# First batch of a frequency-filter and mixer kernel: filter loads on two other queues, tables issued earlier, second token weights added up on GpSimd

## The chip, the cores and the metric

The kernel runs on one core of a Trainium2 chip. The metric is the device time of one execution in microseconds. The engines are TensorE (PE for its matmuls, PEld for its weight loads), VectorE (DVE), ScalarE (ACT), GpSimd (POOL) and SyncE (SP), which only issues DMAs here. ACT and POOL can issue DMAs too; the issue stands in the engine's own instruction stream. "SPq", "ACTq" and "POOLq" are issues on these engines' queues.

## The reference

Eight batches `x[b]` of 3008 rows by 256 columns. Each is filtered in the frequency domain along the rows, then passes a token mixer and a channel mixer. Inputs are given in double precision words of 64 bits where numpy made them so (the four mixer weights); the kernel turns these into 32 bits itself.

```python
X = np.fft.rfft(x, axis=1)
Y = X * (filt_r + 1j * filt_i)[None]
x = np.fft.irfft(Y, n=3008, axis=1)
xt = x.transpose(0, 2, 1)
h = np.maximum(xt @ w_tok1, 0) @ w_tok2        # 3008 -> 256 -> 3008
u = x + h.transpose(0, 2, 1)
out = u + np.maximum(u @ w_ch1, 0) @ w_ch2     # 256 -> 1536 -> 256
```

## The kernel before

**The stages.** One group is one batch. The transform of length 3008 = 47 x 64 is done in two stages of matmuls. For batch 0, `dft(GROUPS[0])` does the following, all on the chip:

- Twelve `a_unit`s (columns in two halves, rows in six chunks) multiply an x tile with the table `wa0` (L518), and ACT copies the result into `turned` (L521). After each six of them `turn_back` transposes that half of `turned` on DVE.
- Eight steps c0 to c7, one for four of the 32 frequencies of the inner transform. In a step, `b_turned(c)` multiplies with the table tile `wb` into two banks; `products(c)` (L676) multiplies both banks with the filter tile `filt` on DVE; `bi_turned(c)` multiplies back with the same `wb` and with `negs`, a negated piece of the table that `negate(c)` (L238) makes on ACT; and ACT copies the result into `turned` again (L662). L505 is the helper `four` which holds the matmuls of both.

After the steps `turn_back` transposes `turned` once more, and PE forms the first token product (`token_sums`, L765). `token_relu` (L841, ACT) takes it up, `u_unit` (L859) multiplies with the second token weights `w2`, and from there on the loop `mix` runs all eight batches through the mixer, with the transforms of the next batch spread between by a table of due places.

**The weights.** The 64-bit weights come as raw words in tiles `st` and are converted by `halves`: ACT scales the upper words (L258), DVE works on the bits (L260, L261, L264, L266), and the two parts `top` and `rest` are added up. Either PE adds them, as two matmuls with an identity-like table (`on_chip`, L304 and L305), and ACT copies the sum out (L307); or `rounded` adds them on DVE (L293). There are 38 such tiles, in this order:

- 12 tiles of the first token weights `w1` (`w1_tile`), all loaded by SP (`i < EARLY`), two halves each. Added by PE.
- 14 tiles of the second token weights, `w2_load(0)` to `w2_load(13)`, seven for each half of the 256 token channels. Tiles 0 to 5 of each seven have 470 columns, the last 188; the target is written with 128 columns between its elements. Loaded by POOL (L340). `BY_PE = 10`: tiles 0 to 9 are added by PE, tiles 10 to 13 by DVE.
- 12 tiles of the channel weights `wc`, loaded by POOL, added by DVE, two of them before `mix` begins.

Each tile is a generator with stages load, ACT's part, DVE's first part, DVE's second part and addition. Four pointers walk over the list: `begin` (load), `copy` (ACT), `middle`, `end`; `convert()` moves the last three by one and begins loads up to five tiles ahead.

**The order.** Everything is written out by hand (`manual_schedule`): the program order on each engine is the order of the calls. In the steps of batch 0 the generator yields four times a step, and two tiles of `w1` are converted per step; then each `convert()` with `w2` tiles goes along with one of four pieces of `token_sums`.

**Loads of batch 0.** All x tiles are issued at first, half by SP, half by POOL. The filter is loaded by `filt_quad(c)`: for the real part `filt_r` and the imaginary part `filt_i`, two rows groups `odd` = 0 and 1, each with one load of 24 rows by two of 256 (48 KB, L227) and one of 23 rows backwards (46 KB, L230); c0 has the second one in two pieces (L232 and L233). There are three filter tiles `filts` and, for batch 0, two more from the pool `t2`, which are zeroed by POOL. `table_load(c)` loads a table tile of 256 KB (L557) on SP. In before, SP issues in this order: table c0, filter c0 (both parts), the table of c1, then in each step `filt_r` of a step three ahead and the table of a step two ahead, and between them the `w1` tiles. `filt_i` from c1 on is issued by POOL.

Of the kernel before, what the change touches and what calls it, by code (L numbers as in the profile page):

```python
# [14 lines left out]
ALU = mybir.AluOpType  # L15
# [9 lines left out]
K2 = 32  # L25
# [11 lines left out]
KD = 2 * KC  # L37
# [10 lines left out]
MT = 6  # L48
NG = 10
W2G = -(-N2 // NG)  # L50
BY_PE = 10
AP = A // 2
W1S = 7
IN_B = 16
# [74 lines left out]
def kernel(  # L129
# [11 lines left out]
    nc = tc.nc  # L141
# [59 lines left out]
    filts = [glob.tile([P, 2, KC, D], FP32, name="filt%d" % i) for i in range(FB)]  # L201
# [17 lines left out]
    def raw(src, row, ap):  # L219
        return bass.AP(tensor=src.tensor, offset=src.offset + row * D, ap=ap)  # L220

    def filt_quad(c, tiles=filts, queues=(nc.sync, nc.sync)):
        t = tiles[c % len(tiles)]
        for i, (q, src) in enumerate(zip(queues, (filt_r, filt_i))):
            for odd in range(KC):
                k, to = c * KD + odd, odd * HALF
                q.dma_start(t[to:to + A, i], raw(src, k, [[64 * D, A], [KC * D, 2], [1, D]]))  # L227
                down = t[to + 32:to + 32 + A]
                if k:
                    q.dma_start(down[0:A - 1, i], raw(src, 64 - k, [[64 * D, A - 1], [-KC * D, 2], [1, D]]))  # L230
                else:
                    q.dma_start(down[:, i, 0], raw(src, 32, [[64 * D, A], [1, D]]))  # L232
                    q.dma_start(down[0:A - 1, i, 1], raw(src, 64 - KC, [[64 * D, A - 1], [1, D]]))  # L233
# [3 lines left out]
    def negate(c, wb):  # L237
        nc.scalar.activation(out=negs[:, c % 4], in_=wb[:, :, 2], func=AF.Copy, scale=-1.0)  # L238
# [4 lines left out]
    late = [(t2p, "t2"), (t3p, "t3")]  # L243
    stages = [(t4p, "t4")] * (A // 2) + (early * 3)[0:TC * W2G + DH] + late * 5

    def stage(n):
        where, tag = stages.pop(0)
        return where.tile([P, n], I64, tag=tag, name="st")

    def halves(st, n, pair):  # L250

        words = [st.bitcast(t).rearrange("p (n w) -> p n w", w=2)[:, 0:n] for t in (U32, FP32)]
        lo, hi, hi_f = words[0][:, :, 0], words[0][:, :, 1], words[1][:, :, 1]
        top, rest = (v[:, 0:n] for v in pair)
        top_i, rest_i = top.bitcast(U32), rest.bitcast(U32)


        nc.scalar.activation(out=top, in_=hi_f, func=AF.Copy, scale=2.0 ** -112)  # L258
        yield
        nc.vector.tensor_scalar(out=top_i, in0=top_i, scalar1=3, scalar2=None, op0=ALU.logical_shift_left)  # L260
        nc.vector.scalar_tensor_tensor(out=top_i, in0=hi, scalar=0x80000000, in1=top_i,  # L261
                                       op0=ALU.bitwise_and, op1=ALU.bitwise_or)
        yield
        nc.vector.tensor_scalar(out=rest_i, in0=top_i, scalar1=0xFF800000, scalar2=None, op0=ALU.bitwise_and)  # L264

        nc.vector.scalar_tensor_tensor(out=rest, in0=lo, scalar=2.0 ** -52, in1=rest, op0=ALU.mult, op1=ALU.mult)  # L266
        yield top, rest
# [3 lines left out]
    def spare_pair():  # L271
        where, tag = spare[0]
        spare.append(spare.pop(0))
        both = where.tile([P, 2, 512], FP32, tag=tag, name="both")
        return both[:, 0], both[:, 1]
# [3 lines left out]
    def rounded(st, n, parts, late):  # L279
        if late:  # L280

            late_in.reverse()
            where, tag = late_in[0]
            both = where.tile([P, 2, 512], FP32, tag=tag, name="both")
            pair = both[:, 0], both[:, 1]
        else:
            pair = spare_pair()
        h = halves(st, n, pair)
        yield next(h)
        yield next(h)  # L290
        top, rest = next(h)
        for src, dst in parts():
            nc.vector.tensor_tensor(out=dst, in0=src(top), in1=src(rest), op=ALU.add)  # L293


    ended = [0]
# [2 lines left out]
    def on_chip(stat, top, rest, n, parts):  # L299
        banks.append(banks.pop(0))  # L300

        def f(tag=banks[0]):
            ps = bank(tag)
            nc.tensor.matmul(ps[:, 0:n], stat, top, start=True, stop=False)  # L304
            nc.tensor.matmul(ps[:, 0:n], stat, rest, start=False, stop=True)  # L305
            for src, dst in parts:
                nc.scalar.copy(out=dst, in_=src(ps))  # L307

        behind.append(f)

    def w1_tile(i):
        st = stage(512)
        rows = moe_w_tok1.rearrange("(n2 n1) t -> n2 n1 t", n1=N1)
        q = nc.sync if i < EARLY else nc.gpsimd
        last = 2 * i + 2 == A
        if last:
            nc.gpsimd.memset(st.bitcast(U32)[HALF:P, 512:1024], 0)
        for h in range(2):
            n = 1 if last and h else 2
            lo = h * A + 2 * i  # L320
            src = rows[:, lo:lo + n, :]
            if h == 0:
                src = bass.AP(tensor=rows.tensor, offset=rows.offset + (A - 1 - lo) * DT,
                              ap=[[N1 * DT, N2], [-DT, n], [1, DT]])
            q.dma_start(st[h * HALF:(h + 1) * HALF, 0:n * DT].rearrange("p (a t) -> p a t", t=DT), src)
        yield

        h = halves(st, 512, spare_pair())
        yield next(h)
        yield next(h)  # L330
        on_chip(wai_t, *next(h), 512, [(lambda v: v, w1[:, 2 * i:2 * i + 2, :].rearrange("p a t -> p (a t)"))])

    def w2_load(i):

        t, g = divmod(i, W2G)
        nn = min(NG, N2 - g * NG)
        n = nn * N1

        st = stage(512)
        nc.gpsimd.dma_start(st[:, 0:n], moe_w_tok2[ts(t, P), ds(g * NG * N1, n)])  # L340
        yield
        dst = w2[:, t].rearrange("p (a h n2) -> p h n2 a", h=2, n2=HALF)[:, :, ds(g * NG, nn), :]

        def some(h, first, step, w):
            return (lambda v: bass.AP(tensor=v.tensor, offset=v.offset + first, ap=[v.ap[0], [N1, nn], [step, w]]),
                    dst[:, h, :, 0:w])

        parts = [some(0, A - 1, -1, A), some(1, A, 1, A - 1)]
        if i < BY_PE:
            h = halves(st, n, spare_pair())  # L350
            yield next(h)
            yield next(h)
            on_chip(ident, *next(h), n, parts)
        else:
            yield from rounded(st, n, lambda: parts, False)

    def combine(w):
        a11, a12, s4, na22, s3, s2, s1 = (w[:, :, n, :] for n in range(7))
# [22 lines left out]
    def wc2_load(i):  # L381
# [11 lines left out]
        while put_off:  # L393
# [7 lines left out]
    tiles = ([w1_tile(i) for i in range(A // 2)] + [w2_load(i) for i in range(TC * W2G)]  # L401
             + [wc1_load(c * (DC // 512), False) for c in range(DH)] + [f(i) for f, i in LAST])
# [147 lines left out]
    def dft(bs):  # L550
        first = bs[0] == 0
        nb = len(bs)
        tiled = bs not in GROUPS[0:2]
        todo = [(b, c) for b in bs for c in range(NXC // 2 if tiled else NXC)]
        wbs = {}

        def table_load(c):  # L557
            where, tag = (t1p, "t1") if first and c % 5 > 2 else (wbp, "wb")
            wbs[c] = where.tile([P, 2, 4, HALF], FP32, tag=tag, name="wb")
            nc.sync.dma_start(wbs[c], (wbi0_d if first else wbi_d)[:, ts(c, 2)])  # L560
# [4 lines left out]
        def w_load(c):  # L565
            table_load(c)
            filt_quad(c)

        to_load = list(enumerate(todo))

# [40 lines left out]
                    next_sum()  # L611
            yield "w"
        for i, u in enumerate(() if tiled else todo):
            if first and i == 0:
                w_load(0)
            if first and i == 6:
                table_load(1)
            a_unit(*u)
            if bs != GROUPS[1] or i >= XB:
                more(1)  # L620
            yield "a" if i + 1 < len(todo) else "w"
            if first and (i + 1) % (NXC // 2) == 0:

                turn_back(i // (NXC // 2))
# [77 lines left out]
                    w_load(c)  # L702
        yield "w"
        yield "b"
        last = K2 // KD
        if not first:
            for c in range(last):
                pss = b_sets(c)
# [8 lines left out]
                yield "i" if c + 1 == last else "b"  # L717
            bi_sets(last - 1, turn)
            return
        tiles = list(filts)  # L720
        for i in range(2):
            t = t2p.tile([P, 2, KC, D], FP32, tag="t2", name="filt")
            nc.gpsimd.memset(t, 0.0)
            tiles.append(t)

        def filt_next(c):
            if c < last:
                filt_quad(c, tiles, (nc.sync, nc.gpsimd))

        filt_next(1)  # L730
        negate(0, wbs[0])
        filt_next(2)
        pss = b_turned(0)
        for c in range(last):
            products(c, pss, tiles)
            if c + 1 < last:
                pss = b_turned(c + 1)
            bi_turned(c)
            yield
            filt_next(c + 3)  # L740
            yield
            if c + 2 < last:
                table_load(c + 2)
            yield
            if c + 1 < last:
                negate(c + 1, wbs[c + 1])
            yield
# [468 lines left out]
    with tc.manual_schedule():  # L1216
# [29 lines left out]
        parts = [(e, part) for e in range(DH) for part in range(2)]  # L1246
# [33 lines left out]
        n = MT * JP  # L1280
# [58 lines left out]
```

## Time and profile before

| | us |
|---|---|
| median of 3 runs | 2452.27 |
| lowest, highest | 2447.38, 2452.76 |
| profiled execution | 2449.51 |
| its span | 2447.7 |
| PE busy | 2357.9 (96%) |
| DVE busy | 1946.9 (80%) |
| ACT busy | 664.4 (27%) |
| POOL busy | 609.3 (25%) |

The span is the time from the first to the last instruction of the profiled execution; the rest of its time, 1.8 us, lies around it. The granted clock of TensorE in that execution was 0.984 on average. In the windows view each row is one stretch of the span, with the busy time of each engine and the number of its instructions. In the chain and timeline views, the first number is the start in us, the second the length; a bracket tells the idle time before and which engine, line or DMA ended it. In the view of waits, a row tells who waited on what, for how many us in all, in how many places, and the longest one.

The stages of batch 0 in this execution: the last copy of line 521 ends at 21.30; the products of c0 to c7 begin at 28.24, 48.99, 65.69, 76.08, 92.14, 105.16, 116.31 and 122.88; PE works on the token product from 134.8 to 160.9; the relu is at 176.72; and the loop `mix` has begun by 185.

### The profile page before, as it was taken

To read this page: it belongs to the slowest core of one execution; us is meant where nothing else is said; L and a number is where in the kernel's file an instruction comes from. 1 tells how busy PE (TensorE), PEld (TensorE's weight loads), DVE (VectorE), ACT (ScalarE), POOL (GpSimd) and SP (SyncE) were. 2 spreads that over 40 slices of the span, in tenths; PEclk is the share of its full clock that TensorE was granted. 3 is DMA by queue.
4 is the path that set the end of the run, shared out by engine and by line. 5 is a ranking of instruction groups with operands and counts; after the bars stand their busy time and mean duration, and the time that the engine had idled before them with its cause. 6 is when DMAs were issued, how large, how long until landed. Compare 5 with 4: busy or idle time off the path is not lost.

```text
span 2447.7 us, 37536 instructions
## 1 busy us (share of the span) xinstructions
PE 2357.9 (96%) x13436; PEld 1998.9 (82%) x13436; DVE 1946.9 (80%) x3645; ACT 664.4 (27%) x1313; POOL 609.3 (25%) x1047
## 2 busy tenths in 40 slices
PE   3778999999999999999999999999999999999998
PEld 1356788988888888988889888888889888898887
DVE  4579877778887788778887788877887788877786
ACT  2343222232222222132222322222222322212222
POOL 5137535112112311221211121123112212112122
PEclk7899999999999999999999999999999999999999
DMA  7545344633345333533335333443335333431100
GB/s 160 136 127 168 112 132 134 219 122 95 106 127 171 116 92 101 190 112 104 97 116 189 116 90 105 140 160 113 93 103 188 118 97 100 122 128 28 41 14 21
DMA packets 186886, 288.05 MB, mean 118 GB/s; under 512 B 35658, under 2 KB 122612, under 8 KB 186700
## 3 DMA queue, kind: packets, MB, share of 16 engines
q1 hardware_dynamic: 148796, 230.09, 30.0%
q0 software_dynamic: 35008, 52.12, 8.2%
q10 hardware_dynamic: 2896, 3.44, 0.4%
q8 instruction: 106, 1.74, 0.3%
q14 instruction: 80, 0.66, 0.1%
HBM read 205.91 MB, written 79.58 MB: 117 GB/s over the span
## 4 chain that ended last, share of the span: by engine, by line
PE 90%; DVE 4%; issue 1%; ACT 0%; DMA 0%; POOL 0%; DVEq 0%; POOLq 0%; ACTq 0%
PE ps_po L986 35%; PE ps_pg L952 19%; PE ps_pg L968 15%; PE ps_b L505 3%; PE ps_b L816 3%; PE ps_acc L873 3%; PE ps_acc L816 2%; PE ps_b L873 2%; PE ps_pg L505 2%; PE ps_b L851 2%; PE ps_acc L851 2%; PE ps_b L765 1%; DVE t L930 1%; DVE both L261 0%; DVE hh L930 0%
## 5 line engine op out<-in xcount | busy, mean ns | idle before, releaser
L994 POOL DMA_DIRECT2D out_dram<-r x752 | 408.9, 551 | 1450.6 <-issue 817.5
L973 ACT ACTIVATE hh<-hh 128x512 f32<-128x512 f32 (+1 forms) x576 | 347.7, 621 | 1013.8 <-DVE hh L930 1009.9
L930 DVE TENSOR_TENSOR hh<-ps_pg,s 128x512 f32<-128x512 f32 (+3 forms) x864 | 481.9, 585 | 170.8 <-ACT s L955 160.8
L986 PE MATMUL ps_po<-t,wc 128*128 128x256 f32 (+1 forms) x2296 | 558.0, 380 | 0.7 <-DVE t L930 0.7
L986 PEld LDWEIGHTS ps_po<-t,wc 128*128 128x128 f32 x2296 | 427.9, 190 | 95.2 <-issue 38.7
L952 PE MATMUL ps_pg<-v,wc 128*128 128x256 f32 (+1 forms) x1728 | 413.6, 375 | 0.1
L986 PE MATMUL ps_po<-hh,wc 128*128 128x256 f32 (+1 forms) x1722 | 411.5, 375 | 0.6 <-POOL wc L364 0.6
L952 PEld LDWEIGHTS ps_pg<-v,wc 128*128 128x128 f32 x1728 | 328.8, 190 | 38.5 <-POOL wc L363 0.7
L986 PEld LDWEIGHTS ps_po<-hh,wc 128*128 128x128 f32 x1722 | 326.8, 190 | 38.5 <-POOL wc L364 1.4
L968 PE MATMUL ps_pg<-u,wc 128*128 128x256 f32 (+1 forms) x1152 | 292.1, 376 | 5.0 <-DVE hh L930 4.9
L930 DVE TENSOR_TENSOR t<-t,hh 128x256 f32<-128x256 f32 (+1 forms) x576 | 245.9, 427 | 19.8
L968 PEld LDWEIGHTS ps_pg<-u,wc 128*128 128x128 f32 x1152 | 217.2, 190 | 36.3 <-DVE hh L930 10.3
L930 DVE TENSOR_TENSOR s<-ps_pg,hh 128x512 f32<-128x512 f32 (+1 forms) x288 | 196.1, 681 | 30.7 <-DVE hh L930 0.9
L955 ACT COPY s<-ps_pg 128x256 f32<-128x256 f32 (+1 forms) x288 | 106.0, 368 | 332.2 <-PE ps_pg L952 331.0
L930 DVE TENSOR_TENSOR t<-hh 128x512 f32<-128x512 f32 (+1 forms) x288 | 194.1, 674 | 0.6 <-ACT hh L973 0.6
L952 PE MATMUL ps_pg<-u,wc 128*128 128x256 f32 (+1 forms) x576 | 169.9, 377 | 4.2 <-DVE hh L930 4.2
L968 PE MATMUL ps_pg<-v,wc 128*128 128x256 f32 (+1 forms) x576 | 169.2, 375 | 0.0
L952 PEld LDWEIGHTS ps_pg<-u,wc 128*128 128x128 f32 x576 | 108.3, 190 | 19.9 <-DVE hh L930 7.8
L968 PEld LDWEIGHTS ps_pg<-v,wc 128*128 128x128 f32 x576 | 109.2, 190 | 13.0
L676 DVE TENSOR_TENSOR p<-ps_acc,filt 128x1024 f32<-128x1024 f32 x64 | 77.7, 1214 | 33.9 <-PE ps_b L505 21.6
L930 DVE TENSOR_TENSOR u<-ps_acc,u 128x256 f32<-128x256 f32 (+1 forms) x84 | 46.1, 549 | 72.9 <-PE ps_acc L873 50.4
L930 DVE TENSOR_TENSOR u<-ps_b,u 128x512 f32<-128x512 f32 (+2 forms) x126 | 74.5, 591 | 28.9 <-PE ps_b L873 26.7
(153 smaller groups left out, 2640.1 us busy)
## 6 DMA issues: line engine op xcount, KB each, us to landing
w<-w_tmp SPq DMA_DIRECT2D x84, 448.0 KB
w<-w_tmp SPq DMA_DIRECT2D x35, 896.0 KB
out_dram<-r POOLq DMA_DIRECT2D x696, 32.0 KB, 3.5
g_tmp<-t SPq DMA_DIRECT2D x224, 96.0 KB
t<-g_tmp SPq DMA_DIRECT2D x42, 512.0 KB
t<-z_tmp SPq DMA_DIRECT2D x196, 96.0 KB
z_tmp<-t SPq DMA_DIRECT2D x72, 256.0 KB
wb<-wbi_t SPq DMA_DIRECT2D x64, 256.0 KB
```

What stands on the lines that cost most here:

```text
L505: nc.tensor.matmul(outs(i, j), stat(i, j), mov(i, j), start=start, stop=stop)
L676: nc.vector.tensor_tensor(out=prods[c, h], in0=pss[h].unsqueeze(1).to_broadcast([P, 2, 2, D]), in1=tiles[c % len(tiles)], op=ALU.mult)
L816: nc.tensor.matmul(ps[:, at], w[:, n], mov, start=(j == 0 and i in (0, 2)), stop=(j == AP - 1 and i >= 5))
L851: nc.tensor.matmul(ps[:, ds(q * P, n)], t4[b, c][:, r, ts(dh, P)], wai[:, 0:n], start=(first and q == 0), stop=(not first and q == 3))
L873: nc.tensor.matmul(ps[:, ds(j * hw, hw)], h1[:, n, :], w2m[m % 2][:, at, 0:hw], start=(i < 2 and j == 0), stop=(j == len(todo) - 1))
L930: nc.vector.tensor_tensor(out=out, in0=in0, in1=in1, op=op)
L952: nc.tensor.matmul(ps[:, 0:hw], chan[0][:, jp, n, :], mov, start=True, stop=True)
L955: nc.scalar.copy(out=s[:, 0], in_=g[0][:, 0, 0:hw])
L968: nc.tensor.matmul(ps[:, 0:hw], chan[0][:, jp, n, :], mov, start=True, stop=True)
L973: nc.scalar.activation(out=hs, in_=hs, func=AF.Relu)
L986: nc.tensor.matmul(po[i][:, j, 0:hw], chan[1][:, jp, n, :], mov, start=(jp == 0 and first == 1), stop=(jp == JP - 1 and last == 1))
L994: q.dma_start(bass.AP(tensor=ob.tensor, offset=ob.offset + row * D + g * cw, ap=[[N1 * D, 32], [D if h else -D, n], [1, cw]]), blocks[ts(g ...
```

## The change

Three things. First, the constant `BY_PE` goes from 10 to 6, and `rounded` is told by `late=None` to add on GpSimd: so w2 tiles 6 to 13, eight tiles, are added there, and PE adds only tiles 0 to 5. Second, batch 0's filter loads go out with `filt_r` on ScalarE's queue and `filt_i` on GpSimd's, c0's too; and c1's are issued in the middle of the `a_unit`s, no longer after them. Third, the tables of c0 and c1 are issued before the first and the third `a_unit`, c2's before the steps, and then each step issues the table of the step three ahead, on SP, before the filter of the same step.

The lines move a little: in the changed file the products are L684, `table_load`'s DMA L562, the addition of `rounded` L294, the filter loads L227, L230, L232 and L233 as before, and the relu L843.

```diff
-BY_PE = 10
+BY_PE = 6
...
         top, rest = next(h)
+        q = nc.vector if late is not None else nc.gpsimd
         for src, dst in parts():
-            nc.vector.tensor_tensor(out=dst, in0=src(top), in1=src(rest), op=ALU.add)
+            q.tensor_tensor(out=dst, in0=src(top), in1=src(rest), op=ALU.add)
...
-            yield from rounded(st, n, lambda: parts, False)
+            yield from rounded(st, n, lambda: parts, None)
...
+        last = K2 // KD
...
+        tiles = list(filts)
+
+        def filt_next(c):
+            if c < last:
+                filt_quad(c, tiles, (nc.scalar, nc.gpsimd))
...
-            if first and i == 0:
-                w_load(0)
-            if first and i == 6:
-                table_load(1)
+            if first and i in (0, 2):
+                table_load(i // 2)
+            if first and i in (0, 6):
+                filt_next(i // 6)
             a_unit(*u)
...
-        tiles = list(filts)
         for i in range(2):
             t = t2p.tile([P, 2, KC, D], FP32, tag="t2", name="filt")
             nc.gpsimd.memset(t, 0.0)
             tiles.append(t)
 
-        def filt_next(c):
-            if c < last:
-                filt_quad(c, tiles, (nc.sync, nc.gpsimd))
-
-        filt_next(1)
+        table_load(2)
+        filt_next(2)
         negate(0, wbs[0])
-        filt_next(2)
         pss = b_turned(0)
         for c in range(last):
...
             yield
+            if c + 3 < last:
+                table_load(c + 3)
             filt_next(c + 3)
             yield
-            if c + 2 < last:
-                table_load(c + 2)
             yield
```

More of the change, by code (lines that the diff above doesn't have):

```diff
@@ L704, in dft @@
         yield "b"
-        last = K2 // KD
         if not first:
```

## The prediction

> **What bounds the kernel now.** First the windows view, to see where PE is not full (columns: length, busy us of PE, PEld, DVE, ACT, POOL, granted clock, DMA share, GB/s).
>
> ```profile
> 0.00:25.00 25.00, 14.04 (x24) 4.63 (x24) 12.79 (x12) 8.32 (x13) 15.16 (x26) 0.96 0.85 188
> 25.00:125.00 100.00, 55.24 (x404) 28.35 (x404) 50.10 (x73) 25.71 (x62) 25.70 (x34) 0.74 0.59 140
> 125.00:185.00 60.00, 46.11 (x288) 33.30 (x288) 41.27 (x78) 24.92 (x49) 19.88 (x37) 0.91 0.43 121
> 185.00:265.00 80.00, 69.52 (x288) 49.82 (x287) 74.72 (x124) 25.68 (x48) 64.75 (x93) 0.98 0.48 153
> 265.00:2447.00 2182.00, 2172.98 (x12436) 1882.77 (x12436) 1768.05 (x3361) 579.73 (x1141) 483.81 (x859) 1.00 0.37 115
> ```
>
> From 265 us PE is full, so what the prologue saves or loses carries to the end. All edits lie before 185. Between 25 and 125, the eight DFT steps c0 to c7, every engine is half idle. The waits of that stretch, then the start of VectorE's product in some of the steps:
>
> ```profile
> ACT turned L662 <- PE ps_pg L505: 50.2, 6, 21.8
> ...
> PE ps_acc L505 <- DMA wb<-wbi_t: 43.7, 5, 18.4
> ```
> ```profile
> 28.24 1.23 DVE L676 TENSOR_TENSOR p<-ps_acc,filt 128x1024 f32<-128x1024 f32 x1 [2.29 <-PE ps_b L505]
> ...
> 48.99 1.22 DVE L676 TENSOR_TENSOR p<-ps_acc,filt 128x1024 f32<-128x1024 f32 x1 [12.32 <-DMA filt<-in_filt_r_dram]
> ...
> 105.16 1.23 DVE L676 TENSOR_TENSOR p<-ps_acc,filt 128x1024 f32<-128x1024 f32 x1 [2.21 <-PE ps_b L505]
> ...
> 116.31 1.22 DVE L676 TENSOR_TENSOR p<-ps_acc,filt 128x1024 f32<-128x1024 f32 x1
> ...
> 122.88 1.22 DVE L676 TENSOR_TENSOR p<-ps_acc,filt 128x1024 f32<-128x1024 f32 x1
> ```
>
> PE waits for tables, DVE once for a filter. c1 to c5 take (105.16-48.99)/4 = 14.0 us each; c6 to c7, with nothing late, 6.6, which is DVE's own work. So the steps are bound by loads. Now the loads themselves (SyncE's queue, then 5 us of the windows view):
>
> ```profile
> 45.77 2.08 SPq L227 DMA_DIRECT2D filt<-in_filt_r_dram  x1
> 47.89 0.32 SPq L230 DMA_DIRECT2D filt<-in_filt_r_dram  x1
> 48.25 2.21 SPq L227 DMA_DIRECT2D filt<-in_filt_r_dram  x1
> ```
> ```profile
> 45.00:50.00 5.00, 0.32 (x1) 0.00 (x0) 1.00 (x1) 1.34 (x3) 1.97 (x3) 1.00 0.27 69
> ```
>
> A pair of filter loads (94 KB) leaves every 2.4 us, though the DMA engines are 27% busy on average: something narrower than sixteen engines is full. After the steps, the chain of waits:
>
> ```profile
> 160.90 0.79 PE ps_po L304 x2
> ...
> 166.56 1.33 POOL st L372 x3
> ...
> 171.45 4.61 DMA filt<-in_x_dram
> 176.06 0.66 ACT both L258
> 176.72 0.49 ACT h L841
> ```
>
> PE ends the token sums at 160.9, but the relu of line 841 starts at 176.72: it stands on ACT behind the conversion of a channel-weight tile (L258) whose load POOL issued only at 166.56.
>
> **Part 1: the start.** In the changed program ACT issues five filter loads of c0 before its table load (1.28 us), each behind the first x loads (landing 5 to 9 us by the x loads' waits), so the first copy (7.32 now) comes near 10. Then four loads of c1 stand between the sixth and the seventh copy of `turned`; the last needs the semaphore lane of the first half of w1 tile 0. By that landing some 4.3 MB must have moved (x 3.1, c0's filter 0.4, table 0.26, w1 piece 0.26, some of c1); at the 188 GB/s of the first window that is 22 us, where the seventh copy starts at 14.01 now. Six copies at the present 1.1 us follow, so the last ends near 27.5 instead of 21.3: c0 late by 6 us. Nothing covers it (DVE's transposes wait for these copies), unless the loads would have been late anyway.
>
> **Part 2: the loads of the steps.** Removed from SP's queue: 28 loads of filt_r in c1 to c7, and ten of c0. Each cost 0.23 to 0.31 us of issue but up to 3.13 us of blocked queue, with the tables behind them. The tables of c2 and c3 now go out before w1 tile 5. Added to ACT: 33 issues of about 0.33 us (its one DMA issue, wai_t, took 0.34), 1.3 us a step, beside PE's and DVE's work. They wait for landings; behind them on ACT stand two L258 for DVE, the copy L307, `negate` and the next `turned` copies, for which PE and DVE wait. POOL gets five i-loads of c0, 0.6 to 1.1 us each, after its x loads, before the memsets of two tiles; c1's and c2's follow, with 5 us of slack.
>
> If queues were the bound, the floor is DVE: c0 at 34.5, then 7 x 6.9 (products 2.4, two w1 tiles at 2.25 each) puts c7 at 83. [...] The last filter lands near 101, products of c7 at 104: 19 us earlier than 122.88. By the queue reading it is 40 earlier. I take 19, since the even share of c6 and c7 already ran at DVE's pace; the 6 us of part 1 are inside, as the loads go on during it. Ends: 40, and -11 (the rival below).
>
> **Part 3: the w2 tiles.** Tiles 6 to 9 leave PE (four passes of 0.79 us in two rows, 1.6 a tile, 6.3 in all) and ACT (L307, 0.97 a tile); 10 to 13 leave DVE (1.0 a tile). POOL adds eight tiles, six of 240+230 columns and two of 96+92. The nearest row is its own 128x256 add,
>
> ```profile
> L900 POOL TENSOR_TENSOR w<-w 128x256 f32<-128x256 f32 x15 | 12.3, 818 | 18.0 <-DMA w_tmp<-w 14.7 <-PE ps_pg L505 2.5
> ```
>
> 0.82: 6 x 1.64 + 2 x 0.9 = 11.6 us; the write steps over 128 columns, which that row lacks, so up to twice, 23. It spreads over about 20 us in which POOL only issues 0.55 us loads, so it hides; but loads queue behind adds that wait for DVE, the channel tile's above all. What it buys: DVE's conversion of w2 tiles 8 to 13 no longer waits for PE between token sums. From c7's product, DVE is done with transposes at +15.6 and PE puts tile 5 through near +26.5; tiles 8, 9, 10 end at +29, +31, +34, POOL's add at +36, the channel load issues by +38 and lands by +45 (7 to 9 us now), relu at +46 instead of 176.72-122.88 = +53.8. That is 7 us; at most 15 (relu right after the sums at +38), at worst -4 if the strided adds lag.
>
> **Sum.** 19 + 7 = 26 us off the profiled 2449.51: 2423.5. That run lies 2.8 us under the median, so 2426.3.
>
> **Rivals.**
> - Queues, not one engine, were the bound: c7 at 83, 40 + 7 = 47 us, 2405. For: 43.7 us of table waits with tables behind filter loads on SP. Against: the 27% row. 20%.
> - The split does nothing for the steps (same eight semaphore lanes for SP and ACT, nine loads a step): only part 3, 7 us, 2445. 14%.
> - Slower: ACT becomes the bound. All its work stands behind loads for three steps ahead, which wait for w1 loads, which wait for ACT's conversions. It decides where a step from c0 at 34.5 exceeds (122.88-34.5)/7 = 12.6 us; at the 14.2 of today's steps c7 comes at 134, 11 late, and w2 returns 3: 2460. For: 14.0 is what steps cost now. Against: large loads and small ones now mix, so the queue idles less. 9%.
>
> **How the numbers follow.** Likeliest (57%): 2426, its own range 2414 to 2438. The range 2408 to 2447 takes in the second rival and most of the first. What can be told from no change is about 0.2%, 5 us. Faster 0.87, same 0.04, slower 0.09.
>
> **What would show it.** Right: products of c7 (L684 in the changed file) near 104; the wait of PE for wb down from 43.7 us to under 20; last `turned` copy of the first stage near 27; filter loads on ACTq; L294 on POOL under 1.7 us; relu 46 us after c7. Wrong: c7 before 92 (queues were the bound) or after 118 (ACT is), or ACT's waits for filter landings over 6 us in most steps.

## The result and the profile after

Over six runs each, the changed kernel takes 2441.53 us in the median (2438.32 to 2445.08), the kernel before 2451.97 us (2447.38 to 2452.76). The ratio is 0.9961, with a 95% interval of 0.9948 to 0.9974: faster by 6 to 13 us, about 10. The prediction said 26. The profiled execution took 2442.4 us with a span of 2440.6, 7.1 us under the span before.

First the windows view of the changed kernel, with the same stretches and columns as before.

```profile
0.00:25.00 25.00, 10.95 (x16) 3.68 (x16) 9.13 (x8) 4.80 (x7) 16.65 (x29) 0.88 0.86 189
25.00:125.00 100.00, 69.11 (x453) 31.59 (x454) 59.34 (x86) 33.88 (x79) 28.46 (x37) 0.81 0.59 149
125.00:185.00 60.00, 42.86 (x251) 32.63 (x249) 44.80 (x73) 21.40 (x35) 37.24 (x62) 0.89 0.41 124
185.00:265.00 80.00, 70.60 (x296) 52.02 (x296) 73.14 (x122) 24.55 (x46) 60.85 (x88) 0.98 0.47 152
265.00:2440.00 2175.00, 2165.83 (x12408) 1875.83 (x12406) 1765.45 (x3351) 578.42 (x1138) 482.49 (x854) 1.00 0.37 114
```

From 265 us PE is full as before (9.2 us idle, 9.0 before), so the 7.1 us come from the prologue alone. In the first 25 us PE now does less (10.95 us for 14.04), in the next hundred more (69.11 for 55.24). The start became later, the steps faster. Next the waits of the steps, 25 to 125 us:

```profile
DVE both L260 <- ACT both L258: 27.5, 4, 10.7
...
PE ps_pg L506 <- ACT negs L238: 21.7, 4, 9.1
...
ACT both L258 <- DMA filt<-in_filt_r_dram: 14.9, 2, 10.5
...
ACT both L258 <- DMA wb<-wbi_t: 11.1, 1, 11.1
```

PE's 43.7 us behind the tables are gone: the last table now leaves SyncE's queue at 80.20, where it was one of two issued together from 101.45 on (first before, then after).

```profile
101.45 1.00 SPq L560 DMA_DIRECT2D wb<-wbi_t  x2
```
```profile
80.20 0.53 SPq L562 DMA_DIRECT2D wb<-wbi_t  x1
```

In place of these waits DVE waits for ACT's conversions and PE for ACT's `negs`, while ACT waits for landings of filters and tables. Neither is an operand of line 258: that line converts a first weight tile. The timeline of ACT shows what it really does there.

```profile
17.52 0.59 ACT L522 COPY turned<-ps_acc 128x512 f32<-128x512 f32 x1 [0.27 <-PE ps_acc L519]
21.53 0.35 ACTq L227 DMA_DIRECT2D filt<-in_filt_r_dram  x1
...
26.31 0.23 ACTq L230 DMA_DIRECT2D filt<-in_filt_r_dram  x1
26.59 0.59 ACT L522 COPY turned<-ps_b 128x512 f32<-128x512 f32 x1 [8.47 <-DMA st<-in_moe_w_tok_dram]
...
81.46 0.50 ACTq L227 DMA_DIRECT2D filt<-in_filt_r_dram  x1
89.77 0.23 ACTq L230 DMA_DIRECT2D filt<-in_filt_r_dram  x1
90.11 0.66 ACT L258 ACTIVATE both<-st 128x512 f32<-128x512 f32 x1 [10.51 <-DMA filt<-in_filt_r_dram]
```

ACT's issues in the first 130 us took 0.23 to 0.63 us each. But between two issues ACT can stand still: the one at 81.46 takes 0.50 us, and the next goes out only at 89.77. It reuses a completion semaphore (the counter by which a load reports that it has landed), and the load that used it before, ACT's own of 72.30, landed only at 89.75. The trace names the semaphore of each load: SP and ACT take theirs from the same eight (numbers 108 to 112 and 114 to 116 in this kernel), so here a load on the one queue was held by a load of the other. For ACT's issue of 26.31 that was SyncE's load of a first weight tile, issued at 20.26 and landed at 26.29, which the copy does not read. What ACT was held by later is seen in the longest pieces of the chain of waits in this stretch (start, length):

```profile
20.26 6.03 DMA st<-in_moe_w_tok_dram
26.31 13.09 DMA filt<-in_filt_r_dram
39.42 10.04 DMA filt<-in_filt_r_dram
50.08 9.54 DMA wb<-wbi_t
72.30 17.45 DMA filt<-in_filt_r_dram
```

The load issued at 26.31 and the one at 72.30 are 23-row loads of 46 KB; they take 13.09 and 17.45 us to land. The second lands at 89.75, and ACT's issue of 89.77 was waiting for it. Now the products, on DVE:

```profile
41.12 1.22 DVE L684 TENSOR_TENSOR p<-ps_acc,filt 128x1024 f32<-128x1024 f32 x1 [2.11 <-PE ps_b L506]
...
48.09 1.22 DVE L684 TENSOR_TENSOR p<-ps_acc,filt 128x1024 f32<-128x1024 f32 x1
...
95.30 1.22 DVE L684 TENSOR_TENSOR p<-ps_acc,filt 128x1024 f32<-128x1024 f32 x1
...
116.59 1.22 DVE L684 TENSOR_TENSOR p<-ps_acc,filt 128x1024 f32<-128x1024 f32 x1
```

c0 starts at 41.12 (28.24 before), c7 at 116.59 (122.88 before). From c1 to c4 a step still takes (95.30 - 48.09)/3 = 15.7 us, from c4 to c7 7.1, near DVE's own pace (6.6 in before). After the steps, the chain of waits:

```profile
156.46 1.78 POOL w L294 x2
158.24 1.93 POOL st L373 x4
160.18 1.52 POOL w L294 x2
...
168.34 0.59 POOL filt L491
...
169.47 1.47 POOL filt L491 x3
```

and, in the waits from 117 to 187 us, a new one:

```profile
PE ps_pg L954 <- POOL wc L364: 4.3, 1, 4.3
```

The relu starts at 164.06, 47.5 us after c7's products where it was 53.8. But behind it PE waits for the first sums of the channel weights, which stand on POOL behind the w2 additions, channel loads and the twelve x loads of the second batch (L491, 6.7 us).

### The profile page after: what moved, and what is told of

Read it like the earlier page. It is cut to its first block, busy times and chain, and to the rows that moved or that the text cites. A ratio compares the mean times of both kernels' runs of the same rounds, so it can differ in the third digit from the quotient of the medians.

```text
span 2440.6 us, 37494 instructions
## 1 busy us (share of the span) xinstructions
PE 2359.3 (97%) x13420; PEld 1995.8 (82%) x13420; DVE 1951.9 (80%) x3637; ACT 663.0 (27%) x1305; POOL 625.7 (26%) x1068
## 4 chain that ended last, share of the span: by engine, by line
PE 90%; DVE 4%; DMA 3%; POOL 1%; issue 1%; ACT 0%; SPq 0%; ACTq 0%; DVEq 0%; POOLq 0%
PE ps_po L988 35%; PE ps_pg L954 19%; PE ps_pg L970 15%; PE ps_b L506 4%; PE ps_b L818 3%; PE ps_acc L875 3%; PE ps_pg L506 3%; PE ps_acc L818 2%; PE ps_b L875 2%; DMA filt<-in_filt_r_dram 2%; PE ps_b L853 2%; PE ps_acc L853 2%; DVE t L932 1%; DMA wb<-wbi_t 1%; POOL w L294 0%
## 5 line engine op out<-in xcount | busy, mean ns | idle before, releaser
L970 PEld LDWEIGHTS ps_pg<-u,wc 128*128 128x128 f32 x1152 | 217.2, 190 | 37.4 <-DVE hh L932 10.4
L970 PEld LDWEIGHTS ps_pg<-v,wc 128*128 128x128 f32 x576 | 108.9, 190 | 12.9
L684 DVE TENSOR_TENSOR p<-ps_b,filt 128x1024 f32<-128x1024 f32 x64 | 78.3, 1223 | 12.9 <-PE ps_pg L506 11.0
```

Of the source, the lines that this page charges most:

```text
L684: nc.vector.tensor_tensor(out=prods[c, h], in0=pss[h].unsqueeze(1).to_broadcast([P, 2, 2, D]), in1=tiles[c % len(tiles)], op=ALU.mult)
L970: nc.tensor.matmul(ps[:, 0:hw], chan[0][:, jp, n, :], mov, start=True, stop=True)
```

## The experiments

For every kernel three marks are read from its profile: the products of c0 and c7, and the second subtraction of the loop (the first `hh` row of DVE with two instructions; 193.32 before, 185.51 after). The table is in the order of the text; the ratio is to the kernel before on the same chip, with its 95% interval. The runs were made on several chips, on which the kernel before has medians from 2448.45 to 2451.97, so times of different rows are compared by their ratios.

| kernel | c0 | c7 | c0 to c7 | c7 to the loop | span | median | ratio |
|---|---|---|---|---|---|---|---|
| before | 28.24 | 122.88 | 94.6 | 70.4 | 2447.7 | 2451.97 | |
| changed | 41.12 | 116.59 | 75.5 | 68.9 | 2440.6 | 2441.53 | 0.9961 (0.9948 to 0.9974) |
| e1_split | 44.52 | 105.29 | 60.8 | 68.9 | 2428.8 | 2433.28 | 0.9937 (0.9923 to 0.9950) |
| e2_sp | 28.14 | 110.27 | 82.1 | 69.8 | 2433.4 | 2436.49 | 0.9953 (0.9940 to 0.9965) |
| e3_w2 | 28.39 | 122.51 | 94.1 | 68.9 | 2446.6 | 2446.53 | 0.9991 (0.9983 to 1.0000) |
| e4_xsp | 39.65 | 113.74 | 74.1 | 65.0 | 2435.5 | 2437.87 | 0.9954 (0.9941 to 0.9966) |
| e5_before_split | 28.07 | 110.95 | 82.9 | 71.4 | 2438.8 | 2439.10 | 0.9954 (0.9941 to 0.9966) |
| e6_split_sp | 27.99 | 96.93 | 68.9 | 69.6 | 2422.4 | 2424.37 | 0.9894 (0.9880 to 0.9907) |
| e7_c1_later | 31.73 | 117.18 | 85.5 | 69.8 | 2440.0 | 2441.76 | 0.9965 (0.9952 to 0.9977) |
| e8_split_sp_xsp | 27.69 | 96.84 | 69.2 | 64.9 | 2414.2 | 2417.11 | 0.9867 (0.9852 to 0.9882) |
| e9_tables | 27.40 | 113.48 | 86.1 | 70.7 | 2438.7 | 2440.50 | 0.9963 (0.9950 to 0.9975) |
| e10_before_xsp | 27.61 | 122.84 | 95.2 | 71.4 | 2450.4 | 2449.16 | 0.9994 (0.9985 to 1.0003) |
| e11_cut24 | 27.54 | 123.96 | 96.4 | 70.7 | 2449.0 | 2450.24 | 1.0000 (0.9991 to 1.0009) |
| e12_e8_no_w2 | 27.98 | 98.24 | 70.3 | 71.4 | 2422.2 | 2423.54 | 0.9891 (0.9878 to 0.9905) |

A caution on single marks: e4_xsp has the changed kernel's program up to c7, and reached it 2.9 us sooner. Differences in c7 under 3 us mean nothing here.

Three theories stand against each other for the steps. A: the 23-row loads, slow to land (ACT's of 46 KB took 10.5 us from issue in the median in the changed kernel, its 24-row loads of 48 KB 6.2), are the bound. B: ScalarE, blocked at its own DMA issues, is. C: the order of SyncE's queue, tables behind filters and first weights, is.

**e1_split.** In the changed kernel, the loads that ScalarE issues:

```diff
-    q.dma_start(down[0:A - 1, i], raw(src, 64 - k, [[64 * D, A - 1], [-KC * D, 2], [1, D]]))
+    q.dma_start(down[0:16, i], raw(src, 64 - k, [[64 * D, 16], [-KC * D, 2], [1, D]]))
+    q.dma_start(down[16:A - 1, i],
+                raw(src, 64 - k + 16 * 64, [[64 * D, A - 17], [-KC * D, 2], [1, D]]))
```

> The changed kernel, with each 23-row filter load that ScalarE issues cut into one of 16 rows and one of 7; nothing else. [...] Theory B (ScalarE is held by its lanes, whichever load has them; more loads only use more lanes): c7 stays at 113 or later and the time within 4 us of 2441.5.

The time of landing is read from the trace's semaphore events, load by load: uncut, the fifteen loads landed 4.0 to 19.2 us after issue, 10.5 in the median; cut, the two pieces in 5.1 and 4.9, at most 8.9. The same bytes, with more loads in the same eight semaphores, landed in half the time. The number of these events differs with the shape, too: before and after, each 23-row filter load from SP's or ACT's queue has 2 events on its semaphore, each 24-row one 13. The steps took 60.8 us for 75.5, and by the ratios the time fell by about 6 us more than with the change. So the shape of these loads did cost. c7, however, came no sooner than 105.29, and c0 only at 44.52, 3.4 us later than in the changed kernel: ACT still stood 8.7 us between the sixth and seventh copy, now with six issues there instead of four. That is theory B's part, though c7 came before its 113.

**e2_sp.** Real filter loads of the changed kernel back on SyncE:

```diff
-                filt_quad(c, tiles, (nc.scalar, nc.gpsimd))
+                filt_quad(c, tiles, (nc.sync, nc.gpsimd))
```

> The changed kernel, with the real filter loads issued by SyncE in the same places of the program instead of ScalarE. Theory B (ScalarE blocked at its own DMA issues holds conversions and copies): the six copies after the sixth follow at once, c0's products start near 29 for 41.1, no step waits for ScalarE, c7 comes at 103 or earlier, and the time falls by 10 us or more to about 2430. [...]

c0 starts at 28.14, near the 29 expected. c7 comes at 110.27: 6.3 us sooner than with ScalarE's queue, but later than the 103 of B. From c0 to c7 the changed kernel is 6.6 us shorter (75.5 for 82.1), but it starts 13.0 us later, and the loads of its steps go on meanwhile; e7_c1_later shows that this late start is not the price by itself. The times alone do not settle it: the two ratios, 0.9953 and 0.9961, overlap.

**e3_w2.** The kernel before with part 3 alone.

```diff
-BY_PE = 10
+BY_PE = 6
...
+        q = nc.vector if late is not None else nc.gpsimd
         for src, dst in parts():
-            nc.vector.tensor_tensor(out=dst, in0=src(top), in1=src(rest), op=ALU.add)
+            q.tensor_tensor(out=dst, in0=src(top), in1=src(rest), op=ALU.add)
...
-            yield from rounded(st, n, lambda: parts, False)
+            yield from rounded(st, n, lambda: parts, None)
```

> The kernel before with the third part alone: BY_PE 6 and the additions of eight tiles on GpSimd. By the prediction's part 3 the relu comes 46 to 47.5 us after c7's products instead of 53.8, so near 170 for 176.7. If GpSimd's chain from the additions to the first channel weights then sets the start of the mixing loop, as the profile of the changed kernel suggests, of these 7 us some 5 are given back, and the time falls by 1 to 3 us only (2449 to 2451); if nothing is given back, by 7 (2445).

The relu comes at 169.98, 47.5 us after c7, by this distance 6.3 sooner than before; the loop starts 1.5 sooner after c7. The ratio says 0 to 4 us. The rest was given back behind the relu, as expected if POOL's chain holds the loop.

**e4_xsp.** The changed kernel with the second batch's x loads off GpSimd:

```diff
-        ahead[0](XF, nc.gpsimd)
+        ahead[0](XF, nc.sync)
```

> The changed kernel, with the twelve x loads of the second batch that stand on GpSimd ahead of its first channel weight sums (6.7 us, from 168.3 to 174.9) issued by SyncE. If GpSimd's chain holds the start of the mixing loop, the first sums move from 176.9 to about 170.5, the loop's first subtraction from 180.2 to about 175, and the time falls by 4 to 6 us, to about 2436. If what is given back behind the relu lies elsewhere (ScalarE, VectorE), the time stays within 2 us.

From c7 to the loop 65.0 us for 68.9, so 3.9 us of the given-back time were those issues. (With c7 2.9 us earlier, see the caution, the loop began 6.7 us sooner; 5.1 of them are left in the span.) The ratios of the two, 0.9954 and 0.9961, overlap, so the 3.9 us rest on the marks.

**e5_before_split.** The kernel before, with the same cut as in e1_split for the loads that SyncE issues, c0's included.

> The kernel before, with the 23-row filter loads on SyncE's queue cut into 16 and 7 rows for the first batch; nothing of the change. [...] Theory C (the order on SyncE's queue, tables behind filter loads and first weights, sets the pace): c7 stays at 118 or later and the time within 5 us of that of before.

c7 at 110.95, sooner than the 118 of C. The cut alone, without anything of the change, gains as much as the whole change did (0.9954). What is left is in the waits of this kernel from 25 to 125 us:

```profile
PE ps_acc L509 <- DMA wb<-wbi_t: 33.4, 4, 14.5
```

PE still stands 33.4 us behind tables. The 23-row loads cost 11.9 us in c7, not all of the excess.

**e6_split_sp.** Cut, and real filter loads on SyncE, in the changed kernel.

> The changed kernel with both edits, real filter loads issued by SyncE and cut into 16 and 7 rows. If the two gains add (14.7 us off the steps by the cut, c0 at 28 with SyncE), c7 comes at about 95, and by the constant distance of c7 to the end (2323.5 us) the time is near 2420. [...]

c7 at 96.93: the gains add, within 2 us. The time, 2424.37, is 4 us above the forecast, 2 of them from c7 and 2 from the way from there to the end (2325.5 us of the span for 2323.5). Against e1_split this is also the second measurement of ScalarE's queue: with the cut, loads on ScalarE cost 105.29 - 96.93 = 8.4 us.

**e7_c1_later.** The changed kernel with c1's loads behind the copies:

```diff
-            if first and i in (0, 6):
-                filt_next(i // 6)
+            if first and i == 0:
+                filt_next(0)
...
+        filt_next(1)
         table_load(2)
         filt_next(2)
```

> The changed kernel, with c1's filter loads issued after the copies of the first stage (where the kernel before has them) instead of between the sixth and the seventh. If these four loads are what made the start late, the copies follow one another, c0's products start at 32 to 34 for 41.1, and if the loads' own pace then binds, c1 to c7 follow no earlier than before: c7 110 to 117. If they only shift the wait, c0 stays at 39 or later.

c0 came 9.4 us sooner, and c7 not at all (117.18). The products of c0 to c2 show where it went:

```profile
31.73 1.23 DVE L684 TENSOR_TENSOR p<-ps_acc,filt 128x1024 f32<-128x1024 f32 x1 [2.11 <-PE ps_b L506]
...
43.99 1.23 DVE L684 TENSOR_TENSOR p<-ps_acc,filt 128x1024 f32<-128x1024 f32 x1 [5.41 <-DMA wb<-wbi_t]
...
64.14 1.22 DVE L684 TENSOR_TENSOR p<-ps_acc,filt 128x1024 f32<-128x1024 f32 x1
```

c2 is at 64.14, where it was 65.12. So the late start was hidden by later loads and cost nothing that is seen in c7. The blocked issues in the steps did cost: c1 is at 43.99 here and in e2_sp alike, and c7 follows at 117.18 here and at 110.27 there.

**e8_split_sp_xsp.** e6_split_sp and the edit of e4_xsp together.

> As the kernel with both edits, real filter loads on SyncE and cut in two, and in addition the twelve x loads of the second batch on SyncE instead of GpSimd. The start of the mixing loop comes 4 us sooner after c7 (65 for 69 us from c7's products to the second subtraction of the loop), so the time is 4 us under that of the kernel without this edit.

64.9 us from c7 to the loop, and 2417.11: the fastest, 1.2 to 1.5% under the kernel before.

**e9_tables.** The kernel before, with the order of the tables alone changed:

```diff
-            if first and i == 6:
+            if first and i == 2:
                 table_load(1)
...
+        table_load(2)
         filt_next(1)
...
+            if c + 3 < last:
+                table_load(c + 3)
             filt_next(c + 3)
             yield
-            if c + 2 < last:
-                table_load(c + 2)
             yield
```

> The kernel before with the order of the tables alone changed, all on SyncE as before: c1's table at the third unit, c2's before the steps, then each step issues the table of the step three ahead, before the filter of that step. Theory C (tables late behind filter loads and first weights are the second half of the steps' pace): PE's wait for tables falls from 43.7 us to under 20, c7 comes at 110 to 113, near the 110.3 of the kernel with SyncE's filter loads, and the time falls by 10 to 12 us to about 2439. [...]

Its waits from 25 to 125 us:

```profile
ACT both L258 <- DMA st<-in_moe_w_tok_dram: 44.3, 7, 16.8
...
DVE p L676 <- DMA filt<-in_filt_i_dram: 13.9, 1, 13.9
```

PE's wait for tables falls from 43.7 to 2.2 us, c7 comes at 113.48, 9.4 sooner. The wait moves to the first weight tiles, which now land late, but costs less there. The time equals the changed kernel's: one reordering on one queue is worth as much as all three parts together.

**e10_before_xsp.** The edit of e4_xsp in the kernel before.

> The kernel before with the twelve x loads of the second batch on SyncE instead of GpSimd, nothing else. If GpSimd's queue of loads and not the additions of w2 sets the start of the mixing loop, the distance from c7's products to the loop's second subtraction falls from 70.4 to about 66 us without any part of the change, the relu comes earlier than 53.8 us after c7, and the time falls by 4 to 5 us. If PE's and VectorE's additions of w2 set it (the prediction's reading), the distance stays over 69 and the time within 2 us.

Nothing changed: the relu is 53.7 us after c7, the loop 71.4, and the ratio's interval holds 1. Without part 3 the x loads are hidden behind the w2 tiles.

**e11_cut24.** The kernel before with the 24-row loads cut into 16 and 8, the 23-row loads whole.

> Control for the cut: the kernel before, with the 24-row filter loads on SyncE's queue cut into 16 and 8 rows for the first batch and the 23-row loads left whole. As many more loads as with the 23-row loads cut. Theory A (it is the 23-row shape that lands slowly): the 23-row loads still land 8 us or more after their issue, c7 at 121 or later, the time within 4 us of that of before or above it. If cutting as such helps (smaller loads, another spread over the lanes), c7 near 111 as with the other cut.

The 23-row loads land 7.7 us after issue in the median, a little under the 8 expected, at most 13.6; c7 is at 123.96 and the ratio is 1.0000. Cutting as such did nothing here. It is the 23-row shape.

**e12_e8_no_w2.** The fastest kernel without part 3.

> The kernel with the cut, real filter loads and x loads on SyncE, without the third part: BY_PE 10 and the additions on VectorE again. If part 3 is worth what the distances from c7 to the loop say (1.5 us without the x loads moved), the time is 1 to 3 us above 2417. If the move of the x loads makes GpSimd's additions matter more (the relu was 6.3 us sooner with them), it is 5 to 7 us above, near 2423.

71.4 us to the loop, 2423.54 us: 6.4 us slower, 5.9 by the ratios. So part 3 alone is worth 1.5 us, the x loads alone nothing, both together 5.4 (e4_xsp against before) to 6.5 (e8_split_sp_xsp against this kernel), all in us from c7 to the loop: two chains side by side, of which each hides the other's gain.

## Why the prediction was wrong

The direction and the place were right, the size was not: 26 us forecast, about 10 measured (7.1 between the two profiled spans). Of the 26, 19 were to come from c7, which gave 6.3, and 7 from the relu, of which 1.5 reached the loop. These 7.8 us are what the loop began sooner.

- **Part 1, the start.** Sized at 6 us, it was 12.9 (41.12 - 28.24). The reason given, a first weight piece's semaphore, was right; the amount was not, since that piece was itself issued late: SP stood until 20.25, when a 23-row load of c0 landed 10.4 us after its issue. That the late start would lie inside the loads' time was right (e7_c1_later).
- **Part 2, the steps.** This is where it failed. 19 us were forecast for c7, 6.3 came. The 23-row loads were a bound, though not the only one (e5_before_split, with e11_cut24 as control: 11.9 us). The 19 us rest on "the last filter lands near 101, products of c7 at 104". That was the author's estimate, and no run shows the term: by the semaphore events the last filter load landed at 107.33 before and at 109.39 after (106.67 in e4_xsp), so the change hardly moved the end of this work. c7 came 15.6 us behind that landing before and 7.2 after, and the gain lies there. Two other things set when the loads went out and what stood behind them. One is the order on SyncE: the tables of c5 to c7 landed at 103.02 to 108.61 before and by 89.99 after, and the tables' place alone gives 9.4 us with the 23-row loads left whole (e9_tables). The other is ScalarE. The prediction counted 1.3 us of issue a step and named what stands behind the loads, but costed the blocked issues at nothing. They cost 6.3 us of c7 (changed kernel against e2_sp) and 8.4 with the 23-row loads cut (e1_split against e6_split_sp, where the ratios, 0.9937 and 0.9894, are apart too). Roughly: 9.4 for the tables, less 6.3 for ScalarE's queue, and some 3 that no run separates from chance, is the 6.3 that came.
- **Part 3, the w2 tiles.** The relu came 47.5 us after c7 (46 forecast); the additions took 1.82 us a tile where 1.64 to 3.3 were allowed. The sum then stopped at the relu. Its 6.3 us became 1.5 at the loop, because the channel sums stood on POOL behind those same additions and twelve x issues. The step that failed is that the relu's gain was added in full: what is late next was not asked.
- **The rivals.** That queues were the bound, and "ACT becomes the bound", each held a part of the truth. The mechanism of the second decided from c1 to c4 (15.7 us a step, over the 12.6 it named), but not from c4 on (7.1 us a step). The two were weighed as alternatives, though they act on the same lines at once.
- **Its own signs.** PE's wait for tables did fall under 20 us, the loads are on ACTq, the relu is near 46. c7 at 104 and the last copy near 27 (it is at 33.76) were wrong. The additions on POOL took 1.82 us a tile, over the 1.7 named. ACT's waits for landings over 6 us came at the start (8.47, a weight tile) and in two steps (11.13, a table; 10.51, a filter), not in most.

## What to carry to other kernels

Before a DMA is moved to a compute engine's queue, ask not what its issue costs but what it will wait for, and what stands behind it there; ScalarE was busy for 34 of the 100 us of the steps and still held them up, with waits of up to 10.5 us for filter landings. Look at the shape of small loads: here 23 rows in one load took twice as long to land as 16 and 7 in two (10.5 us for 5.1 and 4.9). And follow a saved wait to the point where the stage ends: of two chains side by side, shortening one gave 1.5 us or nothing, both 5.4 or more.

## What the runs showed of the hardware

While POOL added the w2 tiles, DVE's conversions of the same shape took longer (0.71 us for 0.40 in the mean at L264, 0.84 for 0.65 at L261). Before and after, from 125 to 185 us, the groups by shape (busy us, mean ns):

```profile
L264 DVE TENSOR_SCALAR both<-both 128x470 uint32<-128x470 uint32 x10 | 4.0, 400 | 0.1
```
```profile
L264 DVE TENSOR_SCALAR both<-both 128x470 uint32<-128x470 uint32 x8 | 5.7, 709 | 0.0
```

The single instruction takes 0.40 us where POOL does not add and up to 0.91 beside an addition. The whole tile (four instructions, of which L264 is one) takes 3.0 us (146.72 to 149.69, changed) for 2.1 (151.00 to 153.09, before); of the four, L260 stays at 0.40 us there, and L261 goes from 0.65 to 1.04. The runs tie it to part 3: with part 3 alone (e3_w2) the group of L264 has a mean of 649 ns, in the fastest kernel 810 and in the same kernel without part 3 (e12_e8_no_w2) 399. What makes them slower beside an addition, no run here shows.
